# Named PSUM banks, grouped output units and split reciprocals in a two-branch attention kernel on one core

## The chip, the cores and the metric

The kernel runs on one core of one Trainium2 chip. Its time is the device time of one execution in microseconds (us), as the median of several runs; every time below is on that core. The engines are named as in the profile: PE (matmuls), PEld (PE's weight loads), DVE (vector), ACT (scalar), POOL (GpSimd) and SP (the queue that issues most DMAs).

## The reference

Two attention blocks read the same `x` (2048 tokens, width 576) and are mixed by a gate per token. Block A has 32 heads with keys and values of their own, block B has 32 heads that share one key and one value head; a head is 18 wide. Softmax is over the full row of 2048 keys.

```
def reference(A_x, A_wqkv, A_wo, B_x, B_wq, B_wk, B_wv, B_wo, gate_w):
    ...
        scores = jnp.einsum("bhqd,bhkd->bhqk", q, k) * scale
        p = _softmax(scores, axis=-1)
        o = jnp.einsum("bhqk,bhkd->bhqd", p, v)
        return (lambda x, *d: x.transpose(*d))(o, 0, 2, 1, 3).reshape(B, S, D) @ wo
    ...
    x = A_x
    g = _sigmoid((x * gate_w).sum(-1, keepdims=True))
    a = _A_ref(x, A_wqkv, A_wo)
    b = _B_ref(x, B_wq, B_wk, B_wv, B_wo)
    return g * a + (1 - g) * b
```

## The kernel before, in words

The first 277 us project queries, keys and values (and take the first maxima). Then come 64 heads one after the other: heads 0 to 31 are block B's (shared keys in `ksb`, values in `vb`), heads 32 to 63 block A's (`ksa`, `vg`). Last comes a short tail.

A head has 16 steps, one for each tile of 128 keys, and the main loop takes two steps at a time (`T`, `T + 1`): a *pair*. A pair does this:

- eight score matmuls (`step_scores`, L599): 128 keys by 512 queries each, from the lower half of PE's rows (`SB`), into a PSUM bank; ACT takes the exponential into a slot of `pt` (`exps`, L588), one instruction for one bank or for two neighbouring banks together;
- the row maxima that a later head's softmax needs, `LEAD` = 22 steps ahead (`step_max`, L538): 128 queries by 512 keys each, from the upper half of PE's rows (`MB`). For two query tiles there are six ordinary maxima (`m`; DVE reduces a bank, L554), one pair of matmuls `x` and `c` (ACT copies a clipped difference out, L541; DVE adds it and takes the maximum, L544). Two ordinary maxima in neighbouring banks can be reduced by one instruction (L552);
- the products with the values of the pair before (`step_pv`, L614), four at a time in column strips, all into bank 7 (`acc`), as whole tiles (512 queries) or halves (256). They use all of PE's rows.

Scores and maxima use unlike halves of PE's rows. Once a head, DVE copies the sums out (`head_out`, L636), and `max_rows` reduces the maxima of the next head, transposes them and sends them over POOL, a DMA to `m_d` and DMAs back into two rows of `qs` that the score matmuls read.

Tiles of 128 finished rows are normalised by `normalise(t)`, one step of it at the end of each pair (the list `slow`): the reciprocal of the sums is one DVE instruction (L665), then POOL multiplies. When four tiles are ready, `out_proj` runs their part of the output projection as 32 *units*, twelve matmuls and one eviction each (L743; the first set is evicted by ACT, L749, the second by DVE, L751). The first set lies in steps 521 to 857, the second in 942 to 1016.

The order of the work in a pair is written out by hand, as a string for each of the eight pairs of a head: `s` a score, `S` a score whose exponential is joined with the one before, `m` and `N` the same for maxima, `c` and `x` the other two, `p0h`/`p0f`/`p1h`/`p1f` halves or wholes of the two value products, `U` a unit if one is due. There are four sets of strings: `PLAIN`, `ONE` and `TWO` (one or two units in the head) and `EACH` (the second set of units, a unit in nearly every pair). Before, `UNITS` lays the first 32 units into heads 33 to 52, two in twelve of them and one in eight.

Seven PSUM banks hold scores and maxima. Before, `next_s` takes the least recently used of banks 0 to 3, for scores and `x`, and `next_m` that of banks 4 to 6, for the maxima and the units; `restart` puts the rings back at each head. A pair of `m` and `N`, or of `s` and `S`, is joined only if the rings happen to give neighbouring banks in rising order; otherwise each gets its own instruction.

Of the kernel before, what the change touches and what calls it, by code (L numbers as in the profile page):

```python
# [19 lines left out]
S = 2048  # L20
# [29 lines left out]
def gated_mix_kernel(ctx: ExitStack, tc: tile.TileContext, xT, wall, wv, wo, out):  # L50
# [474 lines left out]
    def step_max(u, i, c, low=False, spare=False, join=None):  # L525

        if u not in MX:
            MX[u] = mxs[u] if u < 2 else mxs[2 + u % 3]  # L530
        b = SB if low else MB
        if c == "x":
            k = L["kd", u if u >= H else 0][b:b + 54, :]
        else:
            k = kst(u)[b:b + 54, c * 512:(c + 1) * 512]
        n = next_s() if c == "x" or spare else next_m()
        pm = bk[:, n, :]
        nc.tensor.matmul(pm, qs[u % 3][b:b + 54, i * P:(i + 1) * P], k, start=True, stop=True)  # L538
        if c == "x":
            MX["x", u, i] = lead.tile([P, 512], F32, name="xb", bufs=2)  # L540
            nc.scalar.activation(MX["x", u, i], pm, AF.Relu)  # L541
        elif c == 0 and ("x", u, i) in MX:
            junk = lead.tile([P, 512], BF16, name="junk", bufs=1)
            nc.vector.tensor_tensor_reduce(junk, pm, MX.pop(("x", u, i)), 1.0, -3e38, op0=OP.add, op1=OP.max,  # L544
                                           accum_out=MX[u][:, i, c:c + 1])
        elif join == "first":
            MX["j"] = (n, 4 * i + c)
        elif join == "second":
            n0, c0 = MX.pop("j")
            assert (n, 4 * i + c) == (n0 + 1, c0 + 1)  # L550
            flat = MX[u].rearrange("p i c -> p (i c)")
            nc.vector.tensor_reduce(flat[:, c0:c0 + 2], bk[:, n0:n0 + 2, :], axis=AX.X, op=OP.max)  # L552
        else:
            nc.vector.tensor_reduce(MX[u][:, i, c:c + 1], pm, axis=AX.X, op=OP.max)  # L554
# [25 lines left out]
    def exps(q):  # L580

        if len(q) == 2 and q[0][0] + 1 != q[1][0]:
            exps(q[:1])
            exps(q[1:])
            return
        n, k = q[0][0], len(q)
        t = next_pt(k)
        nc.scalar.activation(L["pt"][:, t[0]:t[0] + k, :], bk[:, n:n + k, :], AF.Exp, scale=SCALE / LIFT ** 2)  # L588
        for (_, key), x in zip(q, t):
            PT[key] = L["pt"][:, x, :]  # L590

    def step_scores(u, i, c, alone=False, x=None, hold=False):
# [3 lines left out]
        n = next_m() if alone and c == 0 else next_s()  # L596
# [55 lines left out]
    def normalise(t, at_end=False):  # L652
# [12 lines left out]
        nc.vector.reciprocal(sm[:n, :], sm[:n, :])  # L665
# [50 lines left out]
    def out_proj(t0, rows, first=False):  # L716
# [13 lines left out]
        yield  # L730
        w = WO[t0]
        for q in range(8):
            if q < 7:
                load(q + 1)
            o = {y: O[q, y] for y in "hl"}
            for s2 in range(2):
                st_ = 2 * q + s2
                for hf in range(2):
                    fp = mid()
                    n = 0  # L740
                    for a, b in PRODS:
                        for t, r in enumerate(rows):
                            nc.tensor.matmul(fp[:, 0:288], o[b][:r, t, s2 * P:(s2 + 1) * P],  # L743
                                             w[a][:r, t, 288 * hf:288 * hf + 288],
                                             start=(n == 0), stop=(n == 3 * nt - 1))
                            n += 1
                    dst = oacc[:, st_, 288 * hf:288 * hf + 288]
                    if first:
                        nc.scalar.activation(dst, fp[:, 0:288], AF.Copy)  # L749
                    else:  # L750
                        nc.vector.tensor_tensor(dst, fp[:, 0:288], dst, op=OP.add)  # L751
                    yield


# [70 lines left out]
    def pull(n):  # L825
        while n > 0 and todo:
            try:
                next(todo[0])
                n -= 1
            except StopIteration:  # L830
                todo.pop(0)
# [24 lines left out]
    for t0, rows, Ta, Tb, Tc in SEG:  # L856
        when(Ta, lambda t0=t0, rows=rows: slow.append(prep_wo(t0, rows)))
        when(Tb - 4, lambda t0=t0, rows=rows: (todo.append(out_proj(t0, rows, first=t0 == 0)), pull(1)))
# [4 lines left out]
    UNITS = {u: (0, 8) if u % 5 in (0, 2, 4) else (0,) for u in range(33, 53)}  # L863
    assert sum(map(len, UNITS.values())) == 32

    def due(T, t0, t1, n):
        if t0 == SEG[0][3]:
            return int(T % 16 in UNITS.get(T // 16, ()))
# [7 lines left out]
    FIRST = "s m s c s m s m s m s m s m s x"  # L876
    PLAIN = ("s m x s c m s p0h m s m s p0h m s s m s p1h p1h",
# [7 lines left out]
    ONE = ("s m s m p0f m s s m m s p1f s x m s s c U",  # L885
# [7 lines left out]
    TWO = ("p0f s m m s N S p1h m s p1h s x s m c s U m s",  # L893
# [7 lines left out]
    EACH = ("p0f m s s m m s p1f m s s x s c U m s m s",  # L901
# [7 lines left out]

    def pair_order(T):  # L910
        n = len(UNITS.get(T // 16, ()))
        return (EACH if T >= SEG[1][3] else TWO if n == 2 else ONE if n else PLAIN)[T % 16 // 2]

# [7 lines left out]
    def steps_pair(T, M, order, units):  # L921

        ops = order.split()
        ns = [n for n, op in enumerate(ops) if op in "sS"]
        nm = [n for n, op in enumerate(ops) if op in "mN"]
        ncm = [n for n, op in enumerate(ops) if op == "c"]
        maxima = [(0, c) for c in range(2, 4)] + [(1, c) for c in range(4)]
        assert len(ns) == 8 and len(nm) == 6 and len(ncm) == 1
        which = {}
        for k, n in enumerate(nm):  # L930
            which[n] = maxima[k]
        if T % 16 == 0:
            restart()
        ring = sorted(range(4, 7), key=lambda n: USED[n])
        at_bank = {n: ring[k % 3] for k, n in enumerate(n for n, op in enumerate(ops) if op in "mNc" or op == "U" and units)}
        joined = {nm[k - 1]: n for k, n in enumerate(nm)
                  if ops[n] == "N" and at_bank[nm[k - 1]] + 1 == at_bank[n]}
        for n, op in enumerate(ops):
            if op in "sS":
                k = ns.index(n)  # L940
                step_scores(*divmod(T + k // 4, 16), k % 4, hold=k < 7 and ops[ns[k + 1]] == "S")
            elif op in "mN":
                e, c = which[n]
                step_max(*divmod(M + e, 16), c, join="second" if n in joined.values() else "first" if n in joined else None)
            elif op == "c":
                step_max(*divmod(M, 16), 0)
            elif op == "x":
                if M + 2 < NSTEP:
                    step_max(*divmod(M + 2, 16), "x")
            elif op == "U":  # L950
                if units > 0:
                    pull(1)
                    units -= 1
# [13 lines left out]
    for T in range(-LEAD, NSTEP + 2, 2):  # L967
# [5 lines left out]
        if M >= 16 and M % 16 == 0 and M // 16 - 1 < NU:  # L973
            max_rows(M // 16 - 1)
        alone = M >= NSTEP
        units = sum(due(t, Tb, Tc, 32) for t in (T, T + 1) for _, _, _, Tb, Tc in SEG)
        if 0 <= T <= TL and not alone:
            steps_pair(T, M, FIRST if T == 0 else pair_order(T), units)
# [92 lines left out]
```

## Time and profile before

| | us |
|---|---|
| median of 3 runs (lowest, highest) | 2644.73 (2644.58, 2645.7) |
| the profiled execution | 2646.39 |
| its span, first to last instruction | 2644.6 |
| busy: PE, DVE, ACT, POOL | 2621.3, 2406.6, 2368.5, 283.0 |
| heads 1 to 31 | 1089.9 |
| heads 33 to 52 | 751.1 |
| heads 59 to 62 | 183.0 |

The granted clock was 0.998 over the span. Heads are told apart by the copies L636, one a head. A matmul's end in the records is modelled and neighbours overlap, so what an instruction occupies of its engine is read from the start of one to the start of the next, and a busy share near 99% does not by itself say which engine is the limit.

### The profile page before, as it was taken

Reading aid. Unit: us, or ns where it says so; the run is one execution under the profiler, and the core shown is the slowest. Engines: PE = TensorE matmul, PEld = TensorE weight load, DVE = VectorE, ACT = ScalarE, POOL = GpSimd, SP = SyncE. Lnnn points to the kernel's source line nnn. Section 1 sums busy time; section 2 is a strip of 40 time slices with the busy share of each in tenths; the row PEclk is TensorE's granted clock in tenths of the full one; section 3 lists DMA queues with packets and bytes.
Section 4 is the critical chain, followed back from the end, with each engine's and each line's share of the span. In section 5 each row is a group of like instructions: output and inputs, shape, how many; then the busy total and the mean of one; then the engine's idle time right before and its main releaser. Section 6 shows DMA issues by size and latency. Waiting matters only on the chain.

```text
span 2644.6 us, 59215 instructions
## 1 busy us (share of the span) xinstructions
PE 2621.3 (99%) x22758; PEld 940.8 (36%) x22758; DVE 2406.6 (91%) x4470; ACT 2368.5 (90%) x4284; POOL 283.0 (11%) x526
## 2 busy tenths in 40 slices
PE   9999999999999999999999999999999999999998
PEld 7788322222222222222222333332333332223444
DVE  8447999999999999999999999999999999998873
ACT  4341899999999999999999999999999999998885
POOL 4640000002001100100110001000200021001000
PEclk9999999999999999999999999999999999999999
DMA  7332000011001100210132113112221212122312
GB/s 204 122 111 82 26 20 19 19 32 48 25 20 47 44 20 18 54 34 17 40 78 83 43 50 89 59 35 60 77 52 51 51 55 66 40 68 89 91 36 95
DMA packets 127305, 150.19 MB, mean 57 GB/s; under 512 B 55456, under 2 KB 94744, under 8 KB 125933
## 3 DMA queue, kind: packets, MB, share of 16 engines
q1 hardware_dynamic: 112593, 119.38, 16.1%
q0 software_dynamic: 8096, 19.30, 2.1%
q10 hardware_dynamic: 6332, 7.71, 0.8%
q8 instruction: 179, 2.93, 0.5%
q14 instruction: 105, 0.86, 0.1%
HBM read 90.80 MB, written 46.45 MB: 52 GB/s over the span
## 4 chain that ended last, share of the span: by engine, by line
PE 91%; DVE 5%; ACT 1%; DMA 1%; issue 1%; SPq 0%; ACTq 0%; POOL 0%; DVEq 0%
PE bk L614 38%; PE bk L538 24%; PE bk L599 17%; PE bk L268 5%; PE bk L743 4%; DVE mx L554 3%; PE bk L319 2%; ACT pt L588 1%; DMA wst<-wall 1%; DVE norm_a L210 0%; DVE junk L544 0%; SPq L56 0%; DVE oacc L816 0%; DVE pl L283 0%; PE bk L626 0%
## 5 line engine op out<-in xcount | busy, mean ns | idle before, releaser
L588 ACT ACTIVATE pt<-bk 128x512 f32<-128x512 f32 (+1 forms) x3566 | 2078.0, 686 | 65.9 <-PE bk L599 45.5
L554 DVE TENSOR_REDUCE mx<-bk 128x1 f32<-128x512 f32 x2858 | 1785.9, 683 | 69.0 <-PE bk L538 38.4
L599 PE MATMUL bk<-qs,ksb 56*128 56x512 f16 x2688 | 798.8, 380 | 1.4 <-ACT pt L588 0.9
L538 PE MATMUL bk<-ksb,qs 54*128 54x512 f16 x2363 | 737.3, 381 | 1.5 <-DVE mx L554 1.3
L614 PE MATMUL bk<-pt,vb 128*19 128x256 f32 (+1 forms) x6656 | 599.5, 435 | 0.1
L614 PE MATMUL bk<-pt,vg 128*19 128x256 f32 (+1 forms) x5464 | 558.8, 482 | 0.0
L538 PEld LDWEIGHTS <-qs 54*128 54x128 f16 x4096 | 290.2, 94 | 613.0 <-issue 530.9
L599 PE MATMUL bk<-qs,ksa 56*128 56x512 f16 x1408 | 403.8, 380 | 3.0 <-ACT pt L588 2.0
L538 PE MATMUL bk<-ksa,qs 54*128 54x512 f16 x1232 | 388.1, 380 | 2.4 <-DVE mx L554 2.1
L544 DVE CUSTOM_DVE_ANT_0 junk<-bk,xb 128x512 bf16<-128x512 f32 x501 | 341.9, 682 | 2.3 <-PE bk L538 1.3
L541 ACT ACTIVATE xb<-bk 128x512 f32<-128x512 f32 x501 | 306.5, 612 | 3.0 <-PE bk L599 0.7
L599 PEld LDWEIGHTS <-ksb 56*128 56x128 f16 x2688 | 199.8, 93 | 298.8 <-issue 255.3
L614 PEld LDWEIGHTS bk<-pt,vb 128*19 128x19 f32 x6656 | 116.3, 97 | 276.1 <-issue 255.7
L564 POOL TENSOR_SCALAR mt<-mt 128x32 f32<-128x32 f32 x64 | 18.4, 288 | 1603.0 <-DVE mt L562 1603.0
L614 PEld LDWEIGHTS bk<-pt,vg 128*19 128x19 f32 x5464 | 93.8, 97 | 219.0 <-issue 214.8
L599 PEld LDWEIGHTS <-ksa 56*128 56x128 f16 x1408 | 100.1, 93 | 191.8 <-issue 158.6
L552 DVE TENSOR_REDUCE mx<-bk 128x2 f32<-128x1024 f32 x118 | 143.5, 1216 | 0.5 <-PE bk L538 0.4
L538 PE MATMUL bk<-kdb,qs 54*128 54x512 f16 x373 | 141.1, 378 | 0.1
L277 ACT ACTIVATE ph<-bk,tv 128x512 f16<-128x512 f32 x56 | 38.1, 686 | 97.8 <-PE bk L268 61.1
L283 DVE SCALAR_TENSOR_TENSOR pl<-bk,tv,ph 128x512 f16<-128x512 f32 x56 | 41.7, 749 | 71.3 <-ACT ph L277 47.7
L268 PE MATMUL bk<-xh,wh 128*128 128x512 f32 (+1 forms) x295 | 85.2, 386 | 0.7 <-ACT xh L361 0.7
L268 PE MATMUL bk<-xh,wl 128*128 128x512 f32 (+1 forms) x295 | 85.2, 386 | 0.0
(146 smaller groups left out, 1333.0 us busy)
## 6 DMA issues: line engine op xcount, KB each, us to landing
qs<-qkh SPq DMA_DIRECT2D x244, 72.0 KB
qs<-qkl SPq DMA_DIRECT2D x122, 72.0 KB
onh<-oh SPq DMA_DIRECT2D x32, 256.0 KB
onl<-ol SPq DMA_DIRECT2D x32, 256.0 KB
oih<-onh SPq DMA_DIRECT2D x16, 512.0 KB
oil<-onl SPq DMA_DIRECT2D x16, 512.0 KB
ot<-oe SPq DMA_DIRECT2D x220, 36.0 KB
qkh<-ph POOLq DMA_DIRECT2D x56, 128.0 KB, 2.1
```

The costliest lines, as they stand in the source:

```text
L268: nc.tensor.matmul(bk[:, fp, a0:b0], w[a][:kr, k, :], X[b][:kr, k, s0 + a0:s0 + b0], start=(n == 0), stop=(n == len(PROJ) - 1), skip_group ...
L283: nc.vector.scalar_tensor_tensor(l, fp, t, h, op0=OP.mult, op1=OP.subtract)
L319: nc.tensor.matmul(fp[:, 0:288], X[b][:kr, k, st_ * P:(st_ + 1) * P], w[a][:kr, k, :], start=(n == 0), stop=(n == len(PROJ) - 1))
L538: nc.tensor.matmul(pm, qs[u % 3][b:b + 54, i * P:(i + 1) * P], k, start=True, stop=True)
L541: nc.scalar.activation(MX["x", u, i], pm, AF.Relu)
L544: nc.vector.tensor_tensor_reduce(junk, pm, MX.pop(("x", u, i)), 1.0, -3e38, op0=OP.add, op1=OP.max, accum_out=MX[u][:, i, c:c + 1])
L552: nc.vector.tensor_reduce(flat[:, c0:c0 + 2], bk[:, n0:n0 + 2, :], axis=AX.X, op=OP.max)
L554: nc.vector.tensor_reduce(MX[u][:, i, c:c + 1], pm, axis=AX.X, op=OP.max)
L588: nc.scalar.activation(L["pt"][:, t[0]:t[0] + k, :], bk[:, n:n + k, :], AF.Exp, scale=SCALE / LIFT ** 2)
L599: nc.tensor.matmul(bk[:, n, :], kst(u)[b:b + 56, i * P:(i + 1) * P], qs[u % 3][b:b + 56, x * 512:(x + 1) * 512], start=True, stop=True)
L614: nc.tensor.matmul(acc[32 * j:32 * j + 19, a:b], v_of(u, i), PT[u, i, j][:, a:b], start=(i == 0 and a == 0), stop=(i == 15), skip_group_ch ...
L743: nc.tensor.matmul(fp[:, 0:288], o[b][:r, t, s2 * P:(s2 + 1) * P], w[a][:r, t, 288 * hf:288 * hf + 288], start=(n == 0), stop=(n == 3 * nt ...
```

## The change: a bank for each matmul, units in groups, four reciprocals

- Each score, maximum and unit in a string now carries the number of its bank, any of 0 to 6 for any of them. `S` and `N` join groups whose banks are neighbours, in whatever order they come; the group is worked on when its last member is there.
- All strings are new. `PLAIN` joins seven pairs of maxima in a head and eight pairs of scores, `TWO` seven and three, `EACH` two and four.
- The first 32 units lie two each in heads 33 to 48; heads 49 to 52 become plain. A unit can be cut: `U4:5` runs five of its twelve matmuls in bank 4, and a later `U4:7` the other seven. `ONE` is not used.
- In `EACH` a unit stands where a `U` is written (seven in eight pairs); it is no longer dealt out by `due`.
- `max_rows` moves from ahead of the sixth pair of a head into it (`R`): to its end in `PLAIN`, to its middle in `TWO` and `EACH`.
- The reciprocal of tiles 0 to 6 is done in four instructions of 32 columns, in four successive pairs.

```diff
-    def step_max(u, i, c, low=False, spare=False, join=None):
+    def step_max(u, i, c, low=False, spare=False, n=None, group=None):
...
-        n = next_s() if c == "x" or spare else next_m()
+        if n is None:
+            n = next_s() if c == "x" or spare else next_m()
+        touch(n)
...
+        elif group:
             flat = MX[u].rearrange("p i c -> p (i c)")
-            nc.vector.tensor_reduce(flat[:, c0:c0 + 2], bk[:, n0:n0 + 2, :], axis=AX.X, op=OP.max)
+            n0, c0 = group[0]
+            nc.vector.tensor_reduce(flat[:, c0:c0 + len(group)], bk[:, n0:n0 + len(group), :], axis=AX.X, op=OP.max)
+        elif group is not None:
+            pass
...
-        nc.vector.reciprocal(sm[:n, :], sm[:n, :])
+        for k in range(4 if t < 7 else 1):
+            cs = slice(32 * k, 32 * k + 32) if t < 7 else slice(0, P)
+            nc.vector.reciprocal(sm[:n, cs], sm[:n, cs])
+            if t < 7:
+                yield
...
+    def piece(n, count=99):
...
+        mms = UNIT["mms"]
+        fp = bk[:, touch(UNIT["n"]), 0:288]
+        for _ in range(min(count, len(mms) - UNIT["at"])):
+            k = UNIT["at"]
+            nc.tensor.matmul(fp, *mms[k], start=(k == 0), stop=(k == len(mms) - 1))
+            UNIT["at"] = k + 1
+        if UNIT["at"] == len(mms):
+            dst = UNIT["dst"]
+            if UNIT["first"]:
+                nc.scalar.activation(dst, fp, AF.Copy)
+            else:
+                nc.vector.tensor_tensor(dst, fp, dst, op=OP.add)
+            UNIT.clear()
...
-    UNITS = {u: (0, 8) if u % 5 in (0, 2, 4) else (0,) for u in range(33, 53)}
+    UNITS = {u: "TWO" for u in range(33, 49)}
...
-    PLAIN = ("s m x s c m s p0h m s m s p0h m s s m s p1h p1h",
-           "m s N s c x s p0f s m s S m p1h m s s m p1h",
+    PLAIN = ("s3 m6 s5 x2 m4 c1 s0 p0h s6 m3 p0h m5 s2 m4 s0 S1 N3 s6 p1h p1h",
+           "s5 m2 N1 s0 c4 x6 s3 p0f s5 m6 s2 S1 m0 p1h m3 s5 s6 m4 p1h",
...
+           "s3 m2 s0 m5 s1 N4 p0h c3 s2 m6 s0 p0h s4 x1 m2 S5 N3 s0 p1f R",
...
-    TWO = ("p0f s m m s N S p1h m s p1h s x s m c s U m s",
+    TWO = ("s0 m4 m6 s3 s2 N5 p0h s0 m1 c3 s4 p0h s2 m6 s0 N5 S1 x4 p1h p1h",
...
+           "s0 c1 s5 m6 U4 m6 s5 s2 x3 s1 m0 p0f m5 s2 m0 s4 s3 m6 p1f",
...
+           "p0f c5 s2 s3 x6 s4 m1 p1f m3 s0 s2 m1 U5:5 m0 s4 s6 m3 m2 s1 U5:7")
...
-    EACH = ("p0f m s s m m s p1f m s s x s c U m s m s",
+    EACH = ("s6 x0 S5 m2 m3 s4 p0f s1 m0 S2 c3 s5 m6 p1f m1 s2 m0 s4",
...
+    def runs(ops, first, more):
+
+        out = []
+        for n, op in enumerate(ops):
+            if op[0] == first:
+                out.append([n])
+            elif op[0] == more:
+                out[-1].append(n)
+        return [sorted(g, key=lambda n: ops[n][1]) for g in out]
...
-        if T % 16 == 0:
-            restart()
...
+            elif k == "R":
+                assert M % 16 == 0
+                max_rows(M // 16 - 1)
+            elif k == "U":
+                piece(int(op[1]), int(op[3:]) if len(op) > 2 else 99)
...
-        if M >= 16 and M % 16 == 0 and M // 16 - 1 < NU:
+        if M >= 16 and M % 16 == 0 and (T < 0 or alone) and M // 16 - 1 < NU:
             max_rows(M // 16 - 1)
```

More of the change, by code (lines that the diff above doesn't have):

```diff
@@ L580, in exps @@
     def exps(q):
[L582 to L585, printed above, removed]
+        q = sorted(q)
         n, k = q[0][0], len(q)
@@ L590, in exps, with step_scores @@
             PT[key] = L["pt"][:, x, :]
-    def step_scores(u, i, c, alone=False, x=None, hold=False):
+    def step_scores(u, i, c, alone=False, x=None, hold=False, n=None):
         x = c if x is None else x
         b = SB
-        n = next_m() if alone and c == 0 else next_s()
+        if n is None:
+            n = next_m() if alone and c == 0 else next_s()
+        touch(n)
         if alone and c % 2:
@@ L738, in out_proj @@
                 for hf in range(2):
[L739 to L752, printed above, removed]
+                    mms = [(o[b][:r, t, s2 * P:(s2 + 1) * P], w[a][:r, t, 288 * hf:288 * hf + 288])
+                           for a, b in PRODS for t, r in enumerate(rows)]
+                    yield mms, oacc[:, st_, 288 * hf:288 * hf + 288], first
+    UNIT = {}
+    def piece(n, count=99):
+        if not UNIT:
+            while todo and not UNIT:
+                try:
+                    UNIT["mms"], UNIT["dst"], UNIT["first"] = next(todo[0])
+                    UNIT["n"], UNIT["at"] = n, 0
+                except StopIteration:
+                    todo.pop(0)
+            if not UNIT:
+                return
+        mms = UNIT["mms"]
[11 more added lines that the diff above has]
+            UNIT.clear()
     END_T = []
@@ L826, in pull @@
         while n > 0 and todo:
[L827 to L831, printed above, removed]
+            piece(next_m())
+            n -= 1
     at = {}
@@ L920, in gated_mix_kernel @@
     LEADS = "mA0 MA1 mA2 MA3 V.A mB0 MB1 mB2 MB3 V.B"
-    def steps_pair(T, M, order, units):
-        ops = order.split()
[L924 to L931, printed above, removed]
-        if T % 16 == 0:
-            restart()
[L934 to L937, printed above, removed]
-        for n, op in enumerate(ops):
[L939 to L947, printed above, removed]
-                if M + 2 < NSTEP:
[L949 to L953, printed above, removed]
@@ new lines, in runs, with steps_pair @@
+    def runs(ops, first, more):
[6 more added lines that the diff above has]
+        return [sorted(g, key=lambda n: ops[n][1]) for g in out]
+    def steps_pair(T, M, order):
+        ops = order.split()
+        sg, mg = runs(ops, "s", "S"), runs(ops, "m", "N")
+        score, maxi, group, last = {}, {}, {}, set()
+        for g in sg:
+            for n in g:
+                score[n] = len(score)
+            last.add(max(g))
+        todo_m = [(0, c) for c in range(2, 4)] + [(1, c) for c in range(4)]
+        for g in mg:
+            for n in g:
+                maxi[n] = todo_m[len(maxi)]
+                group[n] = ()
+            if len(g) == 1:
+                group[g[0]] = None
+            else:
+                m0, c0 = maxi[g[0]]
+                group[max(g)] = [(int(ops[n][1]), 4 * ((M + m0) % 16) + c0) for n in g]
+        assert len(score) == 8 and len(maxi) == 6
+        for n, op in enumerate(ops):
+            k = op[0]
+            if k in "sS":
+                step_scores(*divmod(T + score[n] // 4, 16), score[n] % 4, hold=n not in last, n=int(op[1]))
+            elif k in "mN":
+                e, c = maxi[n]
+                step_max(*divmod(M + e, 16), c, n=int(op[1]), group=group[n])
+            elif k == "c":
+                step_max(*divmod(M, 16), 0, n=int(op[1]))
+            elif k == "x":
+                if M + 2 < NSTEP:
+                    step_max(*divmod(M + 2, 16), "x", n=int(op[1]))
+            elif k == "R":
[3 more added lines that the diff above has]
+                piece(int(op[1]), int(op[3:]) if len(op) > 2 else 99)
@@ L972, in gated_mix_kernel @@
         M = T + LEAD
[L973 removed]
+        alone = M >= NSTEP
+        if M >= 16 and M % 16 == 0 and (T < 0 or alone) and M // 16 - 1 < NU:
             max_rows(M // 16 - 1)
[L975 removed]
         units = sum(due(t, Tb, Tc, 32) for t in (T, T + 1) for _, _, _, Tb, Tc in SEG)
         if 0 <= T <= TL and not alone:
[L978 removed]
+            steps_pair(T, M, FIRST if T == 0 else pair_order(T))
             units = 0
```

21 lines of the change are left out of this document (8 added, 13 removed), and 51 rows, old and new, of tables (EACH, ONE, PLAIN, TWO).

## The prediction

> **What bounds the kernel now.** I read the page first (busy time, then the chain that ended last), then one call of stretches by stage, then stretches of single heads, then the timelines of PE, DVE and ACT within one head.
>
> ```profile
> PE 2621.3 (99%) x22758; PEld 940.8 (36%) x22758; DVE 2406.6 (91%) x4470; ACT 2368.5 (90%) x4284; POOL 283.0 (11%) x526
> ...
> PE 91%; DVE 5%; ACT 1%; DMA 1%; issue 1%; SPq 0%; ACTq 0%; POOL 0%; DVEq 0%
> PE bk L614 38%; PE bk L538 24%; PE bk L599 17%; PE bk L268 5%; PE bk L743 4%; DVE mx L554 3%; PE bk L319 2%; ACT pt L588 1%; DMA wst<-wall 1%; DVE norm_a L210 0%; DVE junk L544 0%; SPq L56 0%; DVE oacc L816 0%; DVE pl L283 0%; PE bk L626 0%
> ```
>
> The chain is PE by 91%: value products (L614), maxima (L538), scores (L599). But DVE and ACT are near full too, so I look at stages (columns: stretch, its length, then busy time of PE, PEld, DVE, ACT, POOL, granted clock, DMA share, GB/s): heads 1 to 31; 33 to 52, in which the first 32 output units lie; 59 to 62, with the second 32; the tail.
>
> ```profile
> 319.00:1408.90 1089.90, 1089.41 (x10418) 305.38 (x10416) 1082.62 (x2020) 1087.76 (x1954) 82.95 (x153) 1.00 0.13 34
> 1443.30:2194.40 751.10, 746.00 (x6454) 239.30 (x6452) 711.67 (x1312) 725.00 (x1316) 53.64 (x99) 1.00 0.21 58
> 2404.40:2587.40 183.00, 181.44 (x1381) 75.30 (x1377) 141.19 (x268) 147.22 (x269) 6.87 (x16) 1.00 0.22 64
> 2587.40:2644.60 57.20, 46.89 (x452) 26.22 (x450) 25.16 (x57) 31.49 (x65) 5.25 (x8) 0.98 0.32 110
> ```
>
> And single heads: a plain one, one with one output unit (33), and two with two units (34, 35), which differ by 1.1 us though they hold the same work.
>
> ```profile
> 1021.80:1056.80 35.00, 35.00 (x338) 9.83 (x336) 34.76 (x66) 34.99 (x64) 0.74 (x3) 1.00 0.07 19
> 1443.30:1479.60 36.30, 36.30 (x334) 11.15 (x330) 34.52 (x64) 35.39 (x64) 0.75 (x3) 1.00 0.19 59
> 1479.60:1517.00 37.40, 37.40 (x322) 12.37 (x320) 35.52 (x68) 36.24 (x67) 0.74 (x3) 1.00 0.19 49
> 1517.00:1555.50 38.50, 37.92 (x318) 12.57 (x314) 36.29 (x70) 36.89 (x69) 0.74 (x3) 1.00 0.20 59
> ```
>
> Busy time counts overlaps, so what an instruction really occupies is read from start to start. On PE:
>
> ```profile
> 1057.58 1.05 PE L614 MATMUL bk<-pt,vb 128*19 128x512 f32 x8
> 1058.57 0.39 PE L599 MATMUL bk<-qs,ksb 56*128 56x512 f16 x1
> ...
> 1059.88 0.39 PE L538 MATMUL bk<-ksb,qs 54*128 54x512 f16 x1
> 1059.88 0.39 PE L599 MATMUL bk<-qs,ksb 56*128 56x512 f16 x1
> 1060.10 0.38 PE L538 MATMUL bk<-ksb,qs 54*128 54x512 f16 x1
> ...
> 1060.41 0.63 PE L614 MATMUL bk<-pt,vb 128*19 128x256 f32 x8
> 1060.97 0.39 PE L599 MATMUL bk<-qs,ksb 56*128 56x512 f16 x1
> ```
>
> ```profile
> 2404.65 0.79 PE L743 MATMUL bk<-woh,oih 128*128 128x288 f32 x4
> ...
> 2406.43 0.39 PE L538 MATMUL bk<-ksa,qs 54*128 54x512 f16 x1
> ```
>
> A score and a maximum start together (1059.88, both): they share what I call a slot, 0.22 us to the next (1060.10). Two scores in a row, or two maxima, need a slot each. From the last slot to a value product are 0.31, so the switch costs 0.09. A product of half a tile (p0h, p1h) takes 0.56 (1060.41 to 1060.97), a whole one (p0f, p1f) 0.99 (1057.58 to 1058.57), an output unit 1.78.
>
> **PE by counting the orders.** For the eight orders of a head I count in their strings slots, switches, halves, wholes and units, at these prices. Old PLAIN: 70 x 0.22 + 25 x 0.09 + 20 x 0.56 + 6 x 0.99 = 34.79. Old ONE: 69, 25, 14, 9 and 1 unit, 35.96. Old TWO: 69, 23, 10, 11 and 2, 37.30. Old EACH: 65, 23, 0, 16 and 7, 44.67. Measured: 35.07, 36.30, 37.40 or 38.50, and 183.0 / 4 = 45.75. What is left over, waiting, is 0.28, 0.34, 0.10 or 1.20, and 1.08. So PE's own work, with little waiting, makes the time, and the new strings can be priced in the same way.
>
> DVE and ACT in the plain head:
>
> ```profile
> 1021.78 0.68 DVE L636 COPY oe<-bk 128x512 f32<-128x512 f32 x1
> 1022.37 1.22 DVE L552 TENSOR_REDUCE mx<-bk 128x2 f32<-128x1024 f32 x1
> 1023.50 0.68 DVE L544 CUSTOM_DVE_ANT_0 junk<-bk,xb 128x512 bf16<-128x512 f32 x1
> ...
> 1024.11 4.87 DVE L554 TENSOR_REDUCE mx<-bk 128x1 f32<-128x512 f32 x8
> ...
> 1039.35 0.22 DVE L560 TENSOR_REDUCE m<-mx 128x16 f32<-128x64 f32 x1
> 1039.67 0.21 DVE L562 STREAM_TRANSPOSE mt<-m 128x32 f32<-128x32 f32 x1
> 1039.82 0.69 DVE L544 CUSTOM_DVE_ANT_0 junk<-bk,xb 128x512 bf16<-128x512 f32 x1
> ...
> 1056.84 0.68 DVE L636 COPY oe<-bk 128x512 f32<-128x512 f32 x1
> ```
>
> ```profile
> 1550.86 1.02 ACT L588 ACTIVATE pt<-bk 128x1024 f32<-128x1024 f32 x1
> 1551.76 0.61 ACT L541 ACTIVATE xb<-bk 128x512 f32<-128x512 f32 x1
> 1552.24 0.62 ACT L588 ACTIVATE pt<-bk 128x512 f32<-128x512 f32 x1
> ```
>
> The head lasts 1056.84 - 1021.78 = 35.06. A reduction of one bank holds DVE (4.87 - 0.68) / 7 = 0.60, a joined one of two banks 1.13, the fused one 0.61, the copy 0.59, the row maxima 0.47. An exponential of one bank holds ACT 0.48, of two 0.90. The old plain head has 44 single and 2 joined reductions: 26.4 + 2.26 + 8 x 0.61 + 0.59 + 0.47 = 34.6 on DVE; 54 singles and 9 joined on ACT are 34.0. All three engines stand within 0.8 us.
>
> **The change, part by part.**
>
> PLAIN (heads 0 to 32 and 49 to 57). PE: 69 slots, 24 switches, 18 halves, 7 wholes: 34.35, less by 0.44. DVE: the fixed banks let 7 pairs be joined in place of 2: ten reductions at 0.60 go, five at 1.13 come, -0.35, to 34.25. ACT: 8 joined in place of 9: +0.06, to 34.1. PE stays the longest. With the same 0.28 of waiting the head takes 34.63. Bounds: 34.35 without any, 35.07 if the bank plan gives all back.
>
> TWO, now in heads 33 to 48. PE: 67 slots, 22 switches, 8 halves, 12 wholes, 2 units: 36.64. DVE as in PLAIN, 34.25. ACT: 66 singles and 3 joined, 34.4, and two evictions of 288 columns, shorter than a single each, so below 35.4. PE is the longest by over a microsecond; I add 0.35 of waiting as in head 33, the nearest row (bounds 0.10 and 1.20, the two old TWO heads): 36.99. The split unit (5 and 7 matmuls) has its extra switch in the count. The 1.20 belongs to heads whose bank ring fell so that no maxima were joined; a named bank makes all heads alike.
>
> EACH: 64 slots, 22 switches, 2 halves, 15 wholes, 7 units: 44.49. Waiting before 1.08, in TWO taken as 0.35: I take 0.8, so 45.3, less by 0.45 a head (bounds 0 and -1.3).
>
> Reciprocals:
>
> ```profile
> L665 DVE RECIPROCAL sm<-sm x9: 942/942/948, 577.7 to 2595.0; 112x128 f32<-112x128 f32 x7, 128x128 f32<-128x128 f32 x1, 96x128 f32<-96x128 f32 x1
> ```
>
> ```profile
> L472 DVE RECIPROCAL g<-g x1: 342/342/342, 229.0 to 229.0; 128x32 f32<-128x32 f32 x1
> ```
>
> One of 0.94 becomes four of 0.34 (the gates' reciprocal has the very size): 1.37 of duration, in four pairs. Heads 1 to 31 hold four of the old and exceed 31 x 35.06 by 3.0, 0.75 each. DVE in a new plain head has 34.63 - 34.25 = 0.4 to spare, so most of the four still shows: I take no change (bounds -0.75 and +0.4 each); in the new TWO heads 2 us to spare hide them, and that gain lies in the sum below. POOL's product, r_d and all later steps come four pairs later. The first reader that could care is the output units' first load at step 517: tile 3 starts at 467 and has its first columns out after nine slow steps, now thirteen, some 30 steps of the loop, so at about 497. Tile 7, which starts at 915 for a load at 938, is not split. Cost: nothing.
>
> Row maxima (R) go from ahead of the sixth pair to its middle or end, past up to seven DVE reductions, 4.3 us. They pass no DMA: the slow steps still come behind the pair.
>
> ```profile
> 1004.28 0.22 DVE L560 TENSOR_REDUCE m<-mx 128x16 f32<-128x64 f32 x1
> ```
>
> ```profile
> 1007.31 1.24 SPq L56 DMA_DIRECT2D qs<-m_d  x2
> ```
>
> ```profile
> qkh<-ph POOLq DMA_DIRECT2D x56, 128.0 KB, 2.1
> ```
>
> The rows are issued 1008.55 - 1004.28 = 4.3 after the maximum, and land some 2.1 later (an estimate, from another queue's median). The head they serve begins a pair (4.4) ahead of its first copy at 1021.78, so at about 1017.4; moved by 4.3, the maximum starts at 1008.6, and 1008.6 + 6.4 = 1015.0: covered by 2.4 us. Without that cover each head would pay what is missing. Cost: nothing.
>
> **Sum.** Heads 1 to 31: 31 x -0.44 = -13.6. Heads 0, 32 and 53 to 57: 7 x -0.44 = -3.1. Heads 33 to 52: 16 x 36.99 + 4 x 34.63 + 0.75 for one reciprocal left in a plain head = 731.1 against 751.1: -20.0. EACH, some 3.6 heads: -1.6. Lead and tail: not touched. Together -38.3. The profiled execution took 2646.39 (span 2644.6 and 1.8 around it), so 2608.1; the median, 2644.73, stands 1.66 lower: 2606.
>
> **Rivals.**
>
> *No waiting left*: every leftover goes to zero but 0.1: 38 x 0.28 + 16 x 0.25 + 3.6 x 0.7 = 17 less, 2589. For it: orders and banks are fixed together. Against: three engines within 0.3 us never ran without waits in any old head. 9%.
>
> *The banks don't free PE in plain heads* (the change does there nothing): 35.07 stays, EACH stays, TWO between 36.99 and 37.84: heads 33 to 52 then sum to 732.9 or 746.5, and the time is 2626 to 2640. For it: DVE, at 34.25, follows PE by 0.1 only. 17%.
>
> *Short returns of a bank* (slower). In the new PLAIN five maxima, in TWO six, use a bank again with only one reduction between; the old ring of three banks always put two between. The round trip:
>
> ```profile
> 1518.98 0.39 PE L538 MATMUL bk<-ksa,qs 54*128 54x512 f16 x1
> ```
>
> ```profile
> 1519.40 3.73 DVE L554 TENSOR_REDUCE mx<-bk 128x1 f32<-128x512 f32 x6 [0.53 <-PE bk L599]
> ```
>
> From matmul to reduction 0.42, the reduction itself 0.68: 1.10 of the 2 x 0.60 there are. If PE has just begun a half product at that moment, DVE loses 0.56 - 0.10 = 0.46. There are 38 x 5 + 16 x 6 = 286 such places; 38.3 / 0.46 = 83 of them, 29%, eat the gain. Caught in half of them: 2606 + 66 = 2672. Against: most of these places have a whole product or several slots ahead of the second use, time in which the bank comes free. 12%.
>
> *The clock.* All stages ran at 1.00, and 0.98 stands only in the tail, where PE was busy 46.89 of 57.20. If new waits thinned PE so much in all heads, 2% of some 2100 us, +42, would end slower, at 2648 or above. PE at 99% speaks against it: 1%. The Trainium skill, "TensorE: Matmul & The Clock Gate", section "A second HAM failure mode: psum-queue depth-cycling", says that going round PSUM banks in each iteration can idle PE in short bursts until its clock gate oscillates; by that rule the sum would be those 2648 or more, but this kernel goes round rings of four and three banks already, and its trace, at 1.00, does not bear the rule out.
>
> **Chances.** Forecast (2590 to 2620) 61%, no waiting 9%, plain unchanged 17%, slower by bank returns or clock 13%. Plus or minus 0.2% (5 us) is what a measurement can tell. Same: 5%, the top of the third and the bottom of the fourth case; slower 12%; faster 83%. The range 2588 to 2633 leaves out the last case and the edges of the others.
>
> **What would show it.** Copies L636 every 34.6 us in plain heads and about 37.0 in heads 33 to 48, all alike; some 380 joined reductions (38 x 7 + 16 x 7) for 118; some 30 reciprocals for 9. Wrong: plain heads at 35.0 or more with waits of DVE for L538 or of PE for reductions; TWO heads above 37.9; a wait of scores for qs<-m_d at each head's start.

## The result and the profile after

The changed kernel takes 2629.22 us (median of four, 2628.63 to 2630.69) against 2644.65 for the kernel before in the same runs: a ratio of 0.9942, 95% interval 0.9924 to 0.9959. It is faster, by 15.4 us, where 38 were forecast.

The page of the changed kernel: the busy times, and the chain that ended last, by engine and by line.

```profile
PE 2608.2 (99%) x22342; PEld 951.7 (36%) x22342; DVE 2387.2 (91%) x4192; ACT 2368.1 (90%) x4408; POOL 282.9 (11%) x526
...
PE 93%; DVE 4%; ACT 1%; DMA 1%; issue 1%; SPq 0%; ACTq 0%; DVEq 0%; POOL 0%
```

ACT stands in the chain with 1%, as before. Nothing in the chain says that ACT matters.

Stretches of the changed kernel in the order of those shown before: heads 1 to 31, 33 to 52, 59 to 62, the tail; then single heads, a plain one, one with two units, one with seven.

```profile
317.90:1404.00 1086.10, 1085.73 (x10170) 310.16 (x10169) 1074.48 (x1878) 1085.31 (x1985) 81.05 (x151) 1.00 0.12 34
1439.50:2182.40 742.90, 741.55 (x6306) 242.96 (x6305) 704.54 (x1214) 725.24 (x1393) 51.65 (x97) 1.00 0.20 58
2395.40:2570.60 175.20, 175.20 (x1387) 74.62 (x1383) 136.54 (x261) 146.05 (x270) 6.89 (x16) 1.00 0.20 61
2570.60:2628.90 58.30, 46.89 (x440) 24.89 (x438) 24.71 (x56) 31.66 (x65) 5.25 (x8) 0.96 0.31 108
1018.60:1053.60 35.00, 35.00 (x332) 10.04 (x329) 34.61 (x62) 35.00 (x65) 0.74 (x3) 1.00 0.07 19
1740.80:1778.40 37.60, 37.54 (x314) 12.66 (x313) 35.26 (x61) 36.55 (x72) 0.74 (x3) 1.00 0.19 59
2439.90:2484.40 44.50, 44.50 (x352) 18.90 (x348) 38.06 (x74) 37.33 (x68) 2.82 (x5) 1.00 0.22 69
```

| stretch | forecast | measured |
|---|---|---|
| heads 1 to 31 | -13.6 | -3.8 |
| heads 33 to 52 | -20.0 | -8.2 |
| lead with head 0; 32; 53 to 57 | -3.1 | -1.1 + 1.2 - 0.8 = -0.7 |
| heads 58 to 62 | -1.6 | +3.8 - 7.8 = -4.0 |
| tail | 0 | +1.1 |

Heads 58 and 59 to 62 belong together: the last pair of head 58 now has two units written in it. Two-unit heads are alike within 0.43 us (37.57 to 38.00), as foretold. So every part of the change was carried out, and in the two long stretches, heads 1 to 31 and 33 to 52, it was worth some three and four tenths of its price.

The joined instructions can be counted in the groups of the changed kernel (count, then busy time and mean ns):

```profile
L555 DVE TENSOR_REDUCE mx<-bk 128x1 f32<-128x512 f32 x2260 | 1424.6, 682 | 68.5 <-PE bk L540 29.4 <-PE bk L599 22.1 <-PE bk L319 1.0
L551 DVE TENSOR_REDUCE mx<-bk 128x2 f32<-128x1024 f32 x417 | 507.1, 1216 | 2.0 <-PE bk L540 1.2 <-issue 0.3
L586 ACT ACTIVATE pt<-bk 128x512 f32<-128x512 f32 x3284 | 1748.7, 624 | 45.8 <-PE bk L599 27.9 <-PE bk L540 11.3
L586 ACT ACTIVATE pt<-bk 128x1024 f32<-128x1024 f32 x406 | 429.2, 1057 | 2.2 <-PE bk L540 1.8 <-PE bk L599 0.3
```

417 reductions are joined (before: 118), but only 406 exponentials (before: 530).

### The profile page after: what moved, and what is told of

Same layout as the page of the kernel before. It is cut to its first block, busy times and chain, and to the rows that moved or that the text cites. A ratio compares the mean times of both kernels' runs of the same rounds, so it can differ in the third digit from the quotient of the medians.

```text
span 2628.9 us, 59506 instructions
## 1 busy us (share of the span) xinstructions
PE 2608.2 (99%) x22342; PEld 951.7 (36%) x22342; DVE 2387.2 (91%) x4192; ACT 2368.1 (90%) x4408; POOL 282.9 (11%) x526
## 4 chain that ended last, share of the span: by engine, by line
PE 93%; DVE 4%; ACT 1%; DMA 1%; issue 1%; SPq 0%; ACTq 0%; DVEq 0%; POOL 0%
PE bk L614 39%; PE bk L599 28%; PE bk L540 15%; PE bk L268 5%; PE bk L764 3%; PE bk L319 2%; DVE junk L546 1%; DVE mx L555 1%; ACT pt L586 1%; DVE norm_a L210 0%; DVE oacc L835 0%; DVE pl L283 0%; PE bk L626 0%; SPq L56 0%; ACT xh L361 0%
## 5 line engine op out<-in xcount | busy, mean ns | idle before, releaser
L555 DVE TENSOR_REDUCE mx<-bk 128x1 f32<-128x512 f32 x2260 | 1424.6, 682 | 68.5 <-PE bk L540 29.4
L540 PE MATMUL bk<-ksb,qs 54*128 54x512 f16 x2363 | 721.3, 380 | 1.1 <-ACT pt L586 0.6
L614 PE MATMUL bk<-pt,vb 128*19 128x256 f32 (+1 forms) x6400 | 593.1, 446 | 0.0
L614 PE MATMUL bk<-pt,vg 128*19 128x512 f32 (+1 forms) x5304 | 550.5, 491 | 0.0
L551 DVE TENSOR_REDUCE mx<-bk 128x2 f32<-128x1024 f32 x417 | 507.1, 1216 | 2.0 <-PE bk L540 1.2
L540 PEld LDWEIGHTS <-qs 54*128 54x128 f16 x4096 | 298.8, 93 | 306.6 <-issue 253.5
L599 PEld LDWEIGHTS <-ksb 56*128 56x128 f16 x2688 | 206.3, 93 | 540.9 <-issue 488.6
L599 PE MATMUL bk<-qs,ksa 56*128 56x512 f16 x1408 | 397.0, 380 | 1.3 <-ACT pt L586 0.5
L540 PE MATMUL bk<-ksa,qs 54*128 54x512 f16 x1232 | 381.6, 380 | 0.6
```

The lines of the kernel that those rows point to most:

```text
L551: nc.vector.tensor_reduce(flat[:, c0:c0 + len(group)], bk[:, n0:n0 + len(group), :], axis=AX.X, op=OP.max)
L599: nc.tensor.matmul(bk[:, n, :], kst(u)[b:b + 56, i * P:(i + 1) * P], qs[u % 3][b:b + 56, x * 512:(x + 1) * 512], start=True, stop=True)
L614: nc.tensor.matmul(acc[32 * j:32 * j + 19, a:b], v_of(u, i), PT[u, i, j][:, a:b], start=(i == 0 and a == 0), stop=(i == 15), skip_group_ch ...
```

## The experiments

All times per head are from copy to copy (`head_out`). Each theory says what holds a plain head at 34.97 in place of 34.63: PE with waits, DVE close behind it, or several engines held together by the banks. A plain head's time is the median of the plain heads. Two copies of the changed kernel, around one such head:

```profile
983.62 0.68 DVE L636 COPY oe<-bk 128x512 f32<-128x512 f32 x1
1018.59 0.68 DVE L636 COPY oe<-bk 128x512 f32<-128x512 f32 x1
```

Totals below are of one run unless said otherwise; the kernel before gave 2644 to 2648 beside them.

### One engine at a time gets less work

`a_act` takes exponentials of 448 of the 512 columns of a bank (the rest of `pt` is a constant), `a_dve` maxima of 448 of 512, `a_pe` products with the values of 7/8 of their columns. What each takes away, as an estimate from start to start of the instructions at both widths, stands in the table.

```diff
a_act  - nc.scalar.activation(L["pt"][:, t[0]:t[0] + k, :], bk[:, n:n + k, :], ...)
       + nc.scalar.activation(L["pt"][:, t[0]:t[0] + k, 0:448], bk[:, n:n + k, 0:448], ...)
a_dve  - nc.vector.tensor_reduce(..., pm, axis=AX.X, op=OP.max)     (and the joined one)
       + nc.vector.tensor_reduce(..., pm[:, 0:448], axis=AX.X, op=OP.max)
a_pe   + e = b - (b - a) // 8
       - nc.tensor.matmul(acc[32 * j:32 * j + 19, a:b], v_of(u, i), PT[u, i, j][:, a:b], ...)
       + nc.tensor.matmul(acc[32 * j:32 * j + 19, a:e], v_of(u, i), PT[u, i, j][:, a:e], ...)
```

> The kernel after, but each exponential covers 448 of the 512 columns of a bank (its output is left short on purpose); ACT is relieved by about 64 x 0.05 = 3.4 us a head, PE and DVE do what they did. Theory A (PE's own work is the limit, as the prediction counted): plain heads stay at 34.97, heads 33 to 48 at 37.6, total within 3 us of 2629. Theory B (PE waits for banks that ACT gives back): plain heads fall towards the DVE and PE counts, 34.3 to 34.5, total 2595 to 2605. Theory C (the three engines hold each other, none alone): 34.8, total 2620 to 2626.

> The kernel after, but each ordinary maximum is reduced over 448 of its 512 columns; DVE is relieved by about 48 x 0.067 = 3.2 us a head. Theory A: nothing moves, total within 3 us of 2629. Theory D (DVE, at 34.25 by count and with joined reductions that hold two banks, is the limit): plain heads 34.4, total about 2607. Theory C: 34.8, 2620 to 2626.

> The kernel after, but the value products leave out the last eighth of their columns (224 of 256, 448 of 512); PE is relieved by about 32 x 0.07 = 2.2 us a head. Theory A: plain heads 34.97 - 2.2, held at about 34.3 by DVE and ACT; heads 33 to 48, where DVE and ACT have 2 us to spare, 37.6 - 2.2 = 35.4; heads 59 to 61 42.3; total 2629 - 38 x 0.6 - 16 x 2.2 - 8 = 2563. Theory B or D: plain heads stay within 0.2 of 34.97.

| | taken away, plain head | plain | two units | 59 to 61 | total |
|---|---|---|---|---|---|
| after | | 34.97 | 37.62 | 44.50 | 2629.22 |
| a_act | ACT 3.4 | 34.77 | 37.44 | 44.48 | 2624.34 |
| a_dve | DVE 3.2 | 34.87 | 37.25 | 44.35 | 2616.32 |
| a_pe | PE 1.7 | 34.77 | 37.09 | 43.97 | 2610.31 |

No engine is *the* limit of a plain head: each relief gives 0.1 to 0.2. PE's gives most in the heads with units, still only 0.5 of some 1.7.

The same cuts made on the kernel before:

> The kernel before, with the value products an eighth narrower, as in a_pe (224 of 256 columns, the last eighth left out); PE relieved by 1.7 us a head. Theory A (before, PE's own work made the time, and only the change ended that): plain heads 35.07 to about 34.6, where DVE stands, heads 59 to 61 from 45.9 to 44.2, total about 2615. Theory C (orders and banks couple the three engines in both kernels, so that no single engine's work is the limit): plain heads fall by 0.2 as in a_pe, total 2625 to 2635.

> The kernel before, with ordinary maxima reduced over 448 of 512 columns; DVE relieved by about 3.2 us a head. If DVE (34.6 by count, the longest beside PE) was a limit before and the joined maxima took it away: plain heads 35.07 to 34.8 or below, total 2630 or below, more than the 0.1 a head of a_dve. Theory C: 0.1 a head, total about 2640. Theory A: nothing.

`b_pe`: plain heads 34.82 for 35.07, total 2619.86. `b_dve`: 35.01, total 2637.76. There too, 1.7 us less of PE's work bought only 0.25.

### All three at once

> The kernel after with all three reliefs at once (exponentials over 448, maxima over 448, value products an eighth narrower; the left-out columns make the output another). One alone gave 0.2 (ACT), 0.1 (DVE), 0.2 (PE) in a plain head. Theory C: together clearly more than the sum 0.5, 1.5 to 1.9 in a plain head (33.1 to 33.4), total 2500 to 2530. Theory E (a fixed latency, neither engine's work: bank round trips and switches): no more than the sum, 34.4, total about 2590.

The copies of a plain head, start of each in the first column:

```profile
976.84 0.69 DVE L639 COPY oe<-bk 128x512 f32<-128x512 f32 x1
1009.61 0.69 DVE L639 COPY oe<-bk 128x512 f32<-128x512 f32 x1
```

32.77, which is 2.20 less; the total is 2501.51. The single reliefs sum to 0.50. So a head gets much shorter only when all three engines have less to do: their work is nearly equal, and the head takes as long as the longest of them, with some waiting on top.

### Two relieved, one left: each engine's own floor

`a_only_pe` is the cuts of `a_act` and `a_dve` together, so that PE alone has its full work; the others likewise. I call the head's time in such a run the floor of the engine that has its full work.

> The kernel after with ACT and DVE both relieved (448 of 512 columns in exponentials and maxima) and PE as it is: PE's own floor. The prediction counted PE at 34.35 in a plain head and 36.64 in TWO. If the count is right and the rest was mutual waiting: plain 34.35 to 34.5, TWO 36.6 to 36.8, total about 2590. If PE's own work was counted too low: 34.7 to 34.8 as in a_act and a_dve alone, TWO 37.2, total about 2613.

> PE and DVE relieved, ACT as it is: ACT's floor, counted 34.1 in a plain head, below 35.4 in TWO. Count right: plain 34.1 to 34.3, TWO 35.4 to 35.9, total about 2570. Counted too low: plain 34.7 as in a_pe, total about 2600.

> PE and ACT relieved, DVE as it is: DVE's floor, counted 34.25 both in plain heads and in TWO. Count right: plain 34.25 to 34.4, TWO about 35.6 as in a_all (which is then a fixed cost), total about 2560. Counted too low, or joined maxima waiting for their second bank: 34.7 as in a_pe and a_act.

> The kernel before with ACT and DVE relieved, PE as it is: PE's floor before, counted 34.79 in a plain head, 35.96 with one unit, 37.30 with two, 44.67 in the last heads. If the count holds: 34.8 to 34.9, 36.0, 37.3 to 37.5, 44.7, total about 2625, and plain heads of a_only_pe lie 0.4 below. If the new orders are not shorter for PE by themselves: the two differ by less than 0.2.

> The kernel before with PE and DVE relieved, ACT as it is: ACT's floor before. If ACT was the hidden limit in both kernels: plain heads 34.6 to 34.8, within 0.15 of the 34.77 after, and the change moved only PE and DVE, which were not the longest. If the new orders raised ACT's waits: 34.1 to 34.4 here, as counted.

> The kernel before with PE and ACT relieved: DVE's floor before, counted 34.6 in a plain head against 34.30 measured after. Count right: 34.55 to 34.7 and 0.3 above after. If joining more maxima moved nothing on DVE itself: 34.3 to 34.4.

Copies around one plain head, of the changed kernel with PE, then ACT, then DVE left as it is:

```profile
973.73 0.69 DVE L637 COPY oe<-bk 128x512 f32<-128x512 f32 x1
1008.00 0.69 DVE L637 COPY oe<-bk 128x512 f32<-128x512 f32 x1
```

```profile
977.39 0.69 DVE L638 COPY oe<-bk 128x512 f32<-128x512 f32 x1
1012.16 0.69 DVE L638 COPY oe<-bk 128x512 f32<-128x512 f32 x1
```

```profile
974.92 0.68 DVE L639 COPY oe<-bk 128x512 f32<-128x512 f32 x1
1009.22 0.68 DVE L639 COPY oe<-bk 128x512 f32<-128x512 f32 x1
```

And of the kernel before, in the same order:

```profile
980.62 0.69 DVE L637 COPY oe<-bk 128x512 f32<-128x512 f32 x1 [0.15 <-PE bk L615]
1015.32 0.69 DVE L637 COPY oe<-bk 128x512 f32<-128x512 f32 x1 [0.15 <-PE bk L615]
```

```profile
976.37 0.69 DVE L638 COPY oe<-bk 128x512 f32<-128x512 f32 x1 [0.18 <-PE bk L616]
1011.08 0.69 DVE L638 COPY oe<-bk 128x512 f32<-128x512 f32 x1 [0.18 <-PE bk L616]
```

```profile
985.70 0.68 DVE L639 COPY oe<-bk 128x512 f32<-128x512 f32 x1
1020.45 0.68 DVE L639 COPY oe<-bk 128x512 f32<-128x512 f32 x1
```

| plain head | PE | ACT | DVE | measured |
|---|---|---|---|---|
| before, counted in the prediction | 34.79 | 34.0 | 34.6 | |
| before, floor | 34.70 | 34.71 | 34.76 | 35.07 |
| after, counted | 34.35 | 34.1 | 34.25 | |
| after, floor | 34.27 | **34.77** | 34.30 | 34.97 |

(The floor of DVE before is the median of the plain heads, 34.76; the pair of rows gives 34.75.) For plain heads this settles it. PE and DVE came out within 0.16 of the counts, and fell by 0.43 and 0.46. ACT's floor is 0.7 above its count in both kernels. Before, all three were equal within 0.06. The change lowered two of them and raised ACT, which has one joined exponential fewer, by 0.06. The highest floor is 34.77 for 34.76. What is left of the gain is a little less waiting over it, 0.20 for 0.31.

| heads with units | PE | ACT | DVE | measured |
|---|---|---|---|---|
| before, head 34 | 37.31 | 36.46 | 36.67 | 37.40 |
| before, head 35 | 38.23 | 37.46 | 37.54 | 38.48 |
| after, two units | 36.91 | 36.72 | 36.91 | 37.62 |
| before, 59 to 61 | 45.6 | 44.2 | 44.7 | 45.9 |
| after, 59 to 61 | 44.28 | 42.92 | 43.9 | 44.50 |

In old head 34 PE was alone at the top and the head ran 0.1 above its floor. In the new heads three floors lie within 0.2, and the head runs 0.7 above the highest (the median of the 16 heads is 37.62). With seven units PE is alone again, 0.4 above DVE, and the head runs 0.22 above its floor.

In a head with units a floor is not the engine's own work alone. DVE has no more to do there than in a plain head, yet its floor is 36.91 for 34.30. A two-unit head of the run in which DVE alone has its full work (busy time of PE, PEld, DVE, ACT, POOL):

```profile
1607.71:1644.61 36.90, 36.90 (x314) 11.99 (x312) 34.99 (x61) 34.03 (x72) 3.80 (x6) 1.00 0.23 63
```

DVE is idle for 1.91 of the 36.90, 1.17 of it in three waits during or within 2 us after the units' matmuls, and PE is idle for none. In the run with ACT's full work ACT waits 0.49 in one such head for the end of a unit. So DVE's and ACT's floors here contain time in which they wait for PE. With all three relieved (`a_all`) a two-unit head still takes 35.59.

### Is it ACT's own work, or what ACT waits for?

ACT's singles and joined ones follow one another after 0.476 and 0.903 us at the shortest; 56 and 8 of them are 33.88 in the new plain head, 0.89 below the floor. If that is waiting for PE or DVE to work something off, it goes when they get far less work. `a_act_pure` halves the width of the products (`e = b - (b - a) // 2`) and reduces 256 of 512 columns: about 7 us less a plain head on PE and 12 on DVE (estimates from start to start; the scores and the maxima themselves stay as they are on PE).

> As a_only_act, but value products cover half of their columns and maxima 256 of 512 (the rest is left out): PE has some 7 us less in a head, DVE some 12. If the 0.9 is waiting behind value products: plain heads 33.9 to 34.1, the sum of ACT's shortest pitches. If it is ACT's own price: 34.7 to 34.8 as in a_only_act.

```profile
975.05 0.69 DVE L638 COPY oe<-bk 128x512 f32<-128x512 f32 x1
1009.83 0.69 DVE L638 COPY oe<-bk 128x512 f32<-128x512 f32 x1
```

Still 34.77 (median of the plain heads; 41.45 in heads 59 to 61, total 2585.53), so the 0.89 does not shrink when PE and DVE have that much less to do. A place in this run where it arises, on ACT and then on PE:

```profile
987.58 0.93 ACT L544 ACTIVATE xb<-bk 128x512 f32<-128x512 f32 x1
...
988.54 0.95 ACT L587 ACTIVATE pt<-bk 128x512 f32<-128x512 f32 x1
...
989.22 1.68 ACT L587 ACTIVATE pt<-bk 128x1024 f32<-128x1024 f32 x2
```

```profile
988.56 0.37 PE L541 MATMUL bk<-ksb,qs 54*128 54x512 f16 x1
988.57 0.39 PE L600 MATMUL bk<-qs,ksb 56*128 56x512 f16 x1
...
988.79 0.38 PE L600 MATMUL bk<-qs,ksb 56*128 56x512 f16 x1
```

The copy of `x` ends at 987.58 + 0.93 = 988.51 and frees its bank (3 in the strings: `x3`, then `m3`). The maximum that takes this bank starts at 988.56, and the two scores behind it in PE's order at 988.57 and 988.79. The joined exponential that reads both starts at 989.22, 0.68 after the one ahead of it in place of 0.48: 0.20 lost by ACT, because ACT frees a bank, PE goes on in order, and ACT needs what stands behind. Start to start, five places of this head lose 0.08 to 0.21 each, 0.62 together, and what is left is lost in smaller steps. 41 matmuls of the head start within 0.06 us after ACT has given back the bank they take (13 in a plain head of the changed kernel). That all of the 0.89 is of this kind was not shown.

### Parts of the change by themselves

`a_mix` spreads the 32 units over heads 33 to 52 as before, two in twelve heads and one in eight, with the new strings (`ONE` too).

```diff
-    UNITS = {u: "TWO" for u in range(33, 49)}
+    UNITS = {u: "TWO" if u % 5 in (0, 2, 4) else "ONE" for u in range(33, 53)}
```

> The kernel after, with the old layout of the first 32 units: heads 33 to 52, twelve with the new TWO strings and eight with the new ONE strings. By the count of the prediction a ONE head costs PE 35.28 to 35.3 and a TWO head 36.64, measured 37.6: if ONE carries the same waiting as TWO (1.0), 36.2, heads 33 to 52 sum to 12 x 37.6 + 8 x 36.2 = 740.8 against 742.9 in the kernel after: total 2627. If ONE runs as clean as the old ONE (0.34 of waiting), 35.6: 736, total 2622. If grouping itself was the gain of this stage: 745 or more.

Heads 33 to 52 take 749.5 against 742.9, the total is 2638.14. The old layout gives back 6.6 of the 8.2 us gained there. A head with one unit costs 36.75, 1.8 over a plain one, while the two units of a new head cost 37.62 - 34.97 = 2.65 together. That is half of the 6.6; the other half is that two-unit heads beside one-unit heads take 37.96 in the mean, for 37.68. And `ONE` joins four pairs of maxima where `TWO` and `PLAIN` join seven, so the 6.6 are of the grouping and of these strings together; a `ONE` with seven was not tried.

`a_nojoin` writes every `N` as `m` in the same bank and order: no maxima are joined.

> The kernel after with the same orders and banks, but no maxima joined: every one reduced by itself as soon as it is there. DVE's count rises by 0.5 a head (seven times 2 x 0.60 - 1.13), to 34.75. If joining is what gained in the plain heads, they go to 35.2 or above, total 2645. If joined maxima cost what they save, by holding two banks while the second matmul is awaited: 34.9 to 35.0, total 2622 to 2632.

A plain head takes 35.13, one with two units 37.72, the total is 2639.73. PE's work is unchanged and lower than before, DVE's is 7 x (2 x 0.60 - 1.13) = 0.5 higher, and the gain in plain heads is gone: 35.13 against 35.07. So the joined maxima, which the new banks allow, carry that gain.

`a_recip` makes the reciprocal one instruction again.

```diff
-        for k in range(4 if t < 7 else 1):
-            cs = slice(32 * k, 32 * k + 32) if t < 7 else slice(0, P)
+        for k in range(1):
+            cs = slice(0, P)
...
-            if t < 7:
-                yield
```

> The kernel after with one reciprocal of 128 columns for each tile again. The prediction gave the split no effect in plain heads and 0.7 in two TWO heads. Measured, heads with a reciprocal exceed their neighbours by 0.22 in place of 0.72. If the split is the reason: heads 7 or 8, 15, 22, 29 and 50 show 0.6 to 0.8 again, total 2632. If DVE's new spare time took it (34.3 for 34.6): 0.2 to 0.4, total 2630.

Four of the five plain heads with a reciprocal exceed the others by 0.55, with four pieces by 0.22. The fifth's pieces spread over heads 29 and 30, which save 0.16 together. The two with two units exceed theirs by 0.55 against 0.06. 4 x 0.33 + 0.16 + 2 x 0.49 = 2.5; the spans of the two profiled executions differ by 2631.3 - 2628.9 = 2.4, and the one total is 2633.11. A piece as it runs in the changed kernel, between reductions:

```profile
576.16 0.34 DVE L667 RECIPROCAL sm<-sm 128x32 f32<-128x32 f32 x1
```

### Can ACT be helped in the same way?

If ACT holds plain heads at 34.77, more joined exponentials should help. `a_join` writes five more pairs of scores in a plain head as joined, at the same banks: ACT's work falls by 5 x (2 x 0.476 - 0.903) = 0.25.

```diff
-  ... m3 s5 s6 m4 p1h      ... s2 c4 s1 x0 p0h s3 m5 s2 m6    s5 m3 s6 ...    ... m2 s0 m5 s1 ...
+  ... m3 s5 S6 m4 p1h      ... s2 c4 S1 x0 p0h s3 m5 S2 m6    s5 m3 S6 ...    ... m2 s0 m5 S1 ...
```

> The kernel after with five more pairs of exponentials joined in PLAIN (13 in place of 8), orders and banks unchanged; ACT's work in a plain head falls by 5 x 0.05 = 0.25. If ACT's work is the limit there: 34.97 to 34.75, total about 2621. If the waits around it are (a joined exponential starts later and holds two banks): 34.95 or more, up to 35.3, total 2629 to 2641.

```profile
1005.76 0.68 DVE L636 COPY oe<-bk 128x512 f32<-128x512 f32 x1
1041.91 0.68 DVE L636 COPY oe<-bk 128x512 f32<-128x512 f32 x1
```

36.15, slower by 1.18 a head; the total is 2680.62 in three rounds, 1.0135 of the kernel before (1.0118 to 1.0152). A joined pair costs some 0.29 (1.18 and the 0.25 of work saved, over five) where the join saves 0.05. The time is lost between ACT's instructions. Taking the shortest time from start to start, 0.476 or 0.903, off each, the head between these two copies loses 0.98 ahead of joined exponentials and 1.54 ahead of ACT's other instructions; the head of the changed kernel shown first loses 0.07 and 1.03. The likely reason is that a pair keeps its first bank from the first score until both have been read, and gives both back late; this was not shown, and other banks for the same pairs were not tried. None of these kernels, with the whole work done, beats the changed one.

## Why the prediction was right and wrong

**Right:** the direction, the counts of PE and DVE in plain heads, two-unit heads all alike, the joined reductions (some 380 foretold, which leaves out heads 49 to 52; 417 found), the row maxima moved into the pair at no cost (no wait of PE for `qs<-m_d` is in the trace) and the range, in its upper part. The head with seven units came out at the price counted for PE, 44.50 for 44.49, and that is luck: PE's floor is 44.28, 0.21 below its count, and 0.22 of waiting stand on it where 0.8 were added.

**The step that failed, plain heads:** "PE stays the longest. With the same 0.28 of waiting the head takes 34.63." PE's price was right by 0.08. But the term for ACT, 34.1, was mis-sized: its floor is 34.77, above the forecast for the whole head. The count priced each instruction at the shortest time from one start to the next and left out the 0.7 to 0.9 that ACT loses between instructions, at the one place that was followed by waiting for scores that stood behind a bank which ACT itself gave back late. A row of the prediction hinted at it: the old ACT was busy 34.99 of 35.00 with a count of 34.0. I put the leftover 0.28 to PE alone, though three engines within 0.8 us by count could each have owned it. 42 plain heads at 0.34 are 14 of the 23 us missing.

**Heads with two units:** "ACT ... below 35.4" and "I add 0.35 of waiting as in head 33". The floors of ACT and DVE are 36.72 and 36.91, not 35.4 and 34.25, and PE's is 36.91 for 36.64. So ACT and DVE were not out of the way: both wait for PE around the units, as shown above, and that wait is not in their counts. Over three nearly equal floors the waiting was 0.71, twice the 0.35. 16 x (37.62 - 36.99) are another 10; heads 58 to 62 gave 2.4 more than forecast, head 32 and the tail took about as much.

**That old heads differ because no maxima were joined** in the slow ones is not borne out: old head 34, with 37.40, has one joined reduction between its copies and head 35, with 38.48, none, and with DVE and ACT relieved head 35 still takes 38.23, 0.93 more than counted for PE. What in its order costs PE this was not tried.

**Reciprocals:** no change was forecast in plain heads; four of the five save 0.33 there, the fifth 0.16. A piece is short, and reductions of both kinds run on around it; whether that is the reason was not tested.

**The rivals.** *The banks don't free PE in plain heads* is nearest, for those heads (0.10 of 0.44) and for the time, which lies inside its 2626 to 2640. But its reason is not borne out: DVE fell with PE, ACT stayed. *Short returns of a bank* was priced for DVE, and with PE and ACT relieved DVE lost next to nothing by them: its floor less its count is 0.16 before and 0.05 after. A wait of the kind was seen at ACT, where the new bank plan lost no more than the old one: ACT's floor less its instructions at the shortest time from start to start is 0.88 before and 0.89 after. *No waiting left* is false: 0.20, 0.71 and 0.22 are left over the highest floor. *The clock* stayed at 1.00 in every stretch of heads. The oscillation that the Trainium skill, "TensorE: Matmul & The Clock Gate", section "A second HAM failure mode: psum-queue depth-cycling", describes for going round banks is not in this trace, though each matmul now names one of seven.

## What to carry to other kernels

Where several engines are busy nearly all the time, neither the chain that ended last nor one engine's count says what a change is worth. Give each engine in turn its full work while the others get less, and take the longest of these floors; an edit pays only down to the next floor. A gain on two engines of three that are level is worth what the third one allows. The waiting on top has to be measured for each order of work: here it was 0.09 to 0.71 a head. It was longest where three floors were nearly equal, but old heads 59 to 61, with PE 0.9 ahead, waited 0.3, as much as old plain heads with three equal floors, so the floors alone do not tell it.

## What was not expected of the hardware

ACT, busy by the records in all of a plain head, has 0.9 us in 35 between its instructions that the smaller loads tried on PE and DVE do not take away. Five more exponentials over two banks each cost 0.29 us a pair and saved 0.05 of work, though the same step on DVE, in banks planned for it, paid (0.07 saved in work a pair, 0.16 a head measured). Four reciprocals of 0.34 us, 1.37 in all, cost a plain head 0.22; one of 0.94 costs 0.55.
